# A hand-written order for the start of a fused kernel's last layer, and earlier rooms for its weights

## The chip, the cores and the metric

The kernel runs on one core of one Trainium2 chip. The metric is the time of one execution in device microseconds (us); the kernel before took 681.94 us (median of three runs, 681.19 to 682.96). A core has a matrix engine (TensorE, PE in the profile; its weight loads are PEld), a vector engine (VectorE, DVE), a scalar engine (ScalarE, ACT), GpSimd (POOL) and SyncE (SP), which here only issues DMAs. Each engine works through its own queue in order and waits at semaphores for the others. PSUM is the memory that PE writes to, SBUF the large working memory.

## The reference

Attention over 4 batches, 8 heads, 576 positions and 64 channels, then a soft mixture of experts, then a layer with the Mish function:

```python
x = attn_out.transpose(0, 2, 1, 3).reshape(2304, 512)
logits = x @ phi                              # 2304 x 32 slots
d = softmax over tokens; slot_input = d.T @ x # 32 x 512, four slots for each of 8 experts
slot_out[e] = relu(slot_input[e] @ w1[e]) @ w2[e]      # 512 -> 1024 -> 512
c = softmax over slots;  x = c @ slot_out     # 2304 x 512
h = x @ w_in                                  # 512 -> 2048
g = h * tanh(softplus(h))                     # Mish
out = g @ w_out                               # 2048 -> 512
```

`w_in` and `w_out` come as 64-bit floats, all else as 32-bit.

## The kernel before

**Stages.** Attention (to about 390 us), in which `w_in` is also converted to 32 bits and parked in DRAM; the experts (to 434 us); the last layer (to the end). The experts' weights are 32 loads of 1 MB, which go into tiles called rooms: `take` gives a room to the next key of a fixed list, `fetch` issues its DMA, `used` is called when the matmuls of a room stand in the program and gives the room to the next key. Rooms lie in the pools `ra` (5), `rd` (9), `rc` (3) and `rb` (`NRB` = 6). Once the experts' keys are all given out, `used` keeps a room of `ra`, and of `ra` alone, for the last layer (L144).

**Experts.** `h_ps` (L810) is the first expert layer, `so_ps` (L843) the second, in four quarters of 32 matmul rows in the profile. Between the quarters `combine` (L821) transposes the combine weights: PE writes `m_ct`, ACT copies it into `ct`, rounded to the matmul's short form, and DVE replaces two of four 32-row stripes by the remainder. So a matmul over 128 rows gives a product of nearly full precision. `so_ps` is then copied by DVE into `so_sb` (in the memory of `si_t`, L853), turned by PE (`m_sot`, L856) and copied by DVE to `s_t` (L857).

**Last layer.** `(c @ slot_out) @ w_in` is computed as `c @ (slot_out @ w_in)`. `inner(j)` makes 256 columns of `slot_out @ w_in`: matmuls `m_wp` (L911), ACT's copy `wp` (L913), a matmul `m_w` that repeats it over four stripes (L915), ACT's copy to `wst` (L917) and DVE's remainder (L918). `mish(u)` is one unit (256 tokens by 256 hidden columns): two matmuls `hp` (L932), Mish on ACT into `gg` (L938), a rounded copy `gh` (L940) and the remainder `gl` on DVE (L941). `second(u)` is that unit's share of the output: 12 matmuls `o_ps` (L957), of `gh` and `gl` with the two parts `wo_h` and `wo_l` of `w_out`. There are 72 units, in three groups of three token blocks by eight column blocks; a group ends with copies `ob` (L962) and stores.

`outer(c)` converts 128 rows of `w_out`, a chunk, from raw 64-bit words: ACT scales the words (L497, L498), DVE makes the number in five instructions (L503, L504, L505, L509, L510), ACT rounds it to `wo_h` (L896), DVE takes the remainder `wo_l` (L897). The 16 chunks are converted during the first group, through four raw buffers.

**What sets the order.** In the attention it is a plan written out; elsewhere a scheduler orders each engine's instructions by its own estimates, except those marked `tc.keep_in_program_order`. The program's text around the change:

```python
LOOK = 4
outer(0); outer(1); inner(0)
for u in range(len(units) + LOOK):
    if u < len(units): mish(u)    # in the first group also loads, outer(..) and inner(j + 1)
    if u >= LOOK: second(u - LOOK)
```

Of the kernel before, what the change touches and what calls it, by code (L numbers as in the profile page):

```python
# [42 lines left out]
def kernel(  # L43
# [23 lines left out]
    NRA, NRB, NRC = 8, 6, 3  # L67
# [28 lines left out]
    rd = late.enter_context(tc.tile_pool(name="rd", bufs=1, side="right"))  # L96
# [666 lines left out]
    ct = p2.tile([128, NT], F32R, name="ct")  # L763
# [56 lines left out]

    def combine(b):  # L821

        for t0, nt in ((0, 4), (4, 1)):
            ps = ps_m.tile([128, nt, 128], F32, tag="m", name="m_ct")
            for j in range(nt):
                for o in range(0, 128, 32):
                    nc.tensor.matmul(ps[o:o + 32, j, :], lhsT=c_all[:, b, t0 + j], rhs=ident, start=True, stop=True)
            n = 512 if nt == 4 else R
            src = ps.rearrange("p t n -> p (t n)")[:, 0:n]
            dst = ct[:, b * S + t0 * 128:b * S + t0 * 128 + n]  # L830
            nc.scalar.copy(dst, src)
            for o in (32, 96):
                nc.vector.tensor_tensor(out=dst[o:o + 32], in0=src[o:o + 32], in1=dst[o:o + 32].bitcast(F32),
                                        op=ALU.subtract)
# [18 lines left out]
    nc.vector.tensor_copy(so_sb, so_ps)  # L853
# [3 lines left out]
    nc.vector.tensor_copy(s_t, ps)  # L857
# [11 lines left out]
    p6 = ctx.enter_context(tc.tile_pool(name="p6", bufs=3, reuse_waits="tile"))  # L869


    raws = []
    for i in range(4):
        if i % 2:
            t = rooms[i][0].tile([128, 2048], U32, tag=rooms[i][1], name="raw")
            raws += [t[:, 0:1024], t[:, 1024:2048]]
        else:
            take(*rooms[i])
    for i in range(2):
        take(p3, f"wi{i}")  # L880

    def load_out(c):

        if c < NFC:
            tc.keep_in_program_order(
                nc.sync.dma_start(out=raws[c % 4], in_=w_out[c * 128:(c + 1) * 128, :].bitcast(U32)))

    def outer(c):

        t = raws[c % 4]  # L890
        w = p6.tile([128, DM], F32, tag="w", name="w", bufs=2)
        sg = p6.tile([128, DM], U32, tag="sg", name="sg", bufs=2)
        scale_words(t)
        high_word(t, sg, w.bitcast(U32))
        low_word(nc.vector, t, sg, w)
        nc.scalar.copy(wo_h[c], w)  # L896
        nc.vector.tensor_tensor(out=wo_l[c], in0=w, in1=wo_h[c].bitcast(F32), op=ALU.subtract)  # L897

    for x in (0, "i0", 1, 2, 3, "i1"):
        if isinstance(x, int):  # L900
            load_out(x)
        else:
            fetch((3, int(x[1]), 0), behind=True)

    def inner(j):

        fb, o = divmod(j * 256, 512)
        wi = parts[3, fb, 0][0].rearrange("p (c f) -> p c f", c=KDM)[:, :, o:o + 256]
        ps = ps_p.tile([128, 256], F32, tag="p", name="m_wp")
        for c in range(KDM):  # L910
            nc.tensor.matmul(ps[32 * c:32 * c + 32, :], lhsT=s_t[:, c, :], rhs=wi[:, c, :], start=True, stop=True)  # L911
        wp = p6.tile([128, 256], F32, tag="wp", name="wp", bufs=2)
        nc.scalar.copy(wp, ps)  # L913
        ps = ps_p.tile([128, 256], F32, tag="p", name="m_w")
        nc.tensor.matmul(ps, lhsT=rr, rhs=wp, start=True, stop=True)  # L915
        dst = wst[:, j * 256:(j + 1) * 256]
        nc.scalar.copy(dst, ps)  # L917
        nc.vector.tensor_tensor(out=dst[64:128], in0=ps[64:128], in1=dst[64:128].bitcast(F32), op=ALU.subtract)  # L918
# [8 lines left out]
    def mish(u):  # L927
        i, j = units[u]
        hp = ps_p.tile([128, 2, 256], F32, tag="p", name="hp")
        for x in range(2):  # L930
            f = 2 * j + x
            nc.tensor.matmul(hp[:, x, :], lhsT=wst[:, f * 128:(f + 1) * 128], rhs=ct[:, i * 256:(i + 1) * 256],  # L932
                             start=True, stop=True)
        hp = hp.rearrange("p a n -> p (a n)")
        gg = p6.tile([128, 512], F32, tag="gg", name="gg")
        gh = p6.tile([128, 512], F32R, tag="gh", name="gh", bufs=LOOK + 1)
        gl = p6.tile([128, 512], F32R, tag="gl", name="gl", bufs=LOOK + 1)
        nc.scalar.activation(out=gg, in_=hp, func=AF.Mish)  # L938
# [7 lines left out]
    def second(u):  # L946
        i, j = units[u]
        gh, gl = gs.pop(u)
        for n in range(2):
            if j == 0:  # L950
                ops[i, n] = ps_o.tile([128, DM], F32, tag="o", name="o_ps")
            ps = ops[i, n]
            for x in range(2):
                f = 2 * j + x
                cols = slice(x * 256 + n * 128, x * 256 + n * 128 + 128)
                for k_, (g_, w_) in enumerate(((gh, wo_h), (gh, wo_l), (gl, wo_h))):
                    nc.tensor.matmul(ps, lhsT=g_[:, cols], rhs=w_[f], start=(j == 0 and x == 0 and k_ == 0),  # L957
                                     stop=(j == NG - 1 and x == 1 and k_ == 2))
            if j == NG - 1:
                ob = p6.tile([128, DM], F32, tag="ob", name="ob", bufs=3)  # L960
                ps = ops.pop((i, n))
                (nc.scalar.copy if n else nc.vector.tensor_copy)(ob, ps)  # L962
                store(2 * i + n, ob)
# [17 lines left out]
    outer(0)  # L981
    outer(1)
    inner(0)
    for u in range(len(units) + LOOK):
        if u < len(units):
            mish(u)
            g, j = units[u][0] // GR, units[u][1]
            i = units[u][0] % GR
            if g == 0:
                if i < 2:  # L990
                    load_out(2 * j + 4 + i)
                if i == 0 and j % 2 == 0 and 2 + j // 2 < NFB:
                    fetch((3, 2 + j // 2, 0), behind=True)
                if j + 1 < NG:
                    if i < 2:
                        outer(2 * j + 2 + i)
                    if i == 1:
                        inner(j + 1)
        if u >= LOOK:
            second(u - LOOK)  # L1000
# [51 lines left out]
```

## Time and profile before

| | |
|---|---|
| median of three runs | 681.94 us |
| the profiled execution | 679.22 us |
| its span in the profile | 677.3 us |
| PE busy | 626.2 us (92%) |
| DVE busy | 404.9 us (60%) |
| ACT busy | 332.7 us (49%) |
| chain that ended last: PE | 77% |
| its line of most time, `o_ps` L957 | 28% |

The span is the time from the first to the last instruction that the profiler recorded on this core. A matmul's recorded duration overlaps with the next matmul's, so the distance of starts (the pitch) tells more than the busy share. The granted clock is the share of full speed, 2.4 GHz, at which TensorE was let run: 1.0, or 0.5 for 1.2 GHz.

### The profile page before, as it was taken

The page shows a single profiled execution, that of the slowest core. Times are in us where ns is not written, and L with a number is a line of the kernel's source. Part 1 is how long each engine was busy: PE and PEld are TensorE (multiplying, and loading weights), DVE is VectorE, ACT ScalarE, POOL GpSimd, SP SyncE. Part 2 cuts the span into 40 slices and gives each one's busy share as a digit, 9 for nine tenths or more (in the row PEclk, how much of TensorE's full clock was granted, in tenths as well). Part 3 has the DMA queues.
Part 4 walks back from the last instruction along what each step waited for, and adds up shares of the span by engine and source line. Part 5 has one row for each costly group of instructions (what it writes and reads, how often), then busy time and mean ns, then how long its engine had stood idle before and what let it go on. Part 6 is the DMA issues. An engine that isn't in the chain of part 4 may idle for free.

```text
span 677.3 us, 11071 instructions
## 1 busy us (share of the span) xinstructions
PE 626.2 (92%) x4002; PEld 461.1 (68%) x4002; DVE 404.9 (60%) x833; ACT 332.7 (49%) x755; POOL 206.8 (31%) x255
## 2 busy tenths in 40 slices
PE   1588899979999999999999998779999999999997
PEld 1565677657677777677677653357787888888885
DVE  6778677784775665656665421599973533343331
ACT  2556766763667656656565301288744321221221
POOL 5659759745675345424300010000000000000000
PEclk9999999998999999999999999969999999999999
DMA  9677689867596775346559579974300300030003
GB/s 265 158 208 186 190 263 270 205 219 199 157 291 183 189 215 130 90 112 172 129 181 315 185 267 379 339 266 164 125 1 0 94 1 0 1 94 0 1 0 94
DMA packets 58454, 107.32 MB, mean 158 GB/s; under 512 B 12704, under 2 KB 25120, under 8 KB 57888
## 3 DMA queue, kind: packets, MB, share of 16 engines
q1 hardware_dynamic: 58400, 106.62, 52.8%
q8 instruction: 32, 0.52, 0.4%
q14 instruction: 22, 0.18, 0.1%
HBM read 69.21 MB, written 8.91 MB: 115 GB/s over the span
## 4 chain that ended last, share of the span: by engine, by line
PE 77%; DMA 7%; DVE 5%; ACT 5%; SPq 2%; issue 2%; POOL 2%; ACTq 0%; DVEq 0%; POOLq 0%
PE o_ps L957 28%; PE m_av L426 14%; PE t L371 8%; PE s L330 5%; PE s L332 4%; PE s L350 3%; DMA w<-in_moe_w_in_dram 3%; PE hp L932 2%; PE so_ps L843 2%; DMA raw<-in_moe_w_out_dram 2%; PE m_lg L452 2%; SPq L185 1%; DMA w<-in_moe_w_dram 1%; PE tk L385 1%; ACT P L364 1%
## 5 line engine op out<-in xcount | busy, mean ns | idle before, releaser
L358 DVE TENSOR_REDUCE nmax<-s 128x1 f32<-128x576 f32 x144 | 108.2, 753 | 66.8 <-PE s L332 38.8
L364 ACT ACTIVATE P<-s,nmax 128x576 f32<-128x576 f32 x144 | 107.3, 745 | 28.2 <-DVE nmax L358 20.5
L957 PE MATMUL o_ps<-wo_h,gh 128*128 128x512 f32 x288 | 114.9, 399 | 0.8 <-ACT gh L940 0.8
L957 PE MATMUL o_ps<-wo_l,gh 128*128 128x512 f32 x288 | 113.9, 396 | 0.0
L957 PE MATMUL o_ps<-wo_h,gl 128*128 128x512 f32 x288 | 108.4, 391 | 0.0
L330 PE MATMUL s<-qk_st 128*128 128x288 f32 x256 | 85.6, 349 | 13.3 <-ACT P L364 7.8
L938 ACT ACTIVATE gg<-hp 128x512 f32<-128x512 f32 x72 | 42.3, 599 | 103.6 <-PE hp L932 100.9
L371 PE MATMUL t<-cs,P 128*128 128x128 f32 x512 | 79.5, 283 | 6.0 <-DVE partl L270 3.3
L407 ACT COPY PT<-t 128x512 f32<-128x512 f32 x93 | 54.2, 586 | 53.4 <-PE t L371 53.0
L371 PEld LDWEIGHTS t<-cs,P 128*128 128x128 f32 x512 | 59.9, 144 | 23.1 <-issue 11.6
L426 PE MATMUL m_av<-PT,w 128*64 128x320 f32 (+1 forms) x384 | 73.1, 421 | 0.9 <-ACT PT L396 0.6
L332 PE MATMUL s<-k_st,qk_st 128*128 128x288 f32 x256 | 73.4, 301 | 0.0
L330 PEld LDWEIGHTS s<-qk_st 128*128 128x128 f32 x256 | 49.7, 194 | 31.0 <-ACT P L364 11.5
L940 DVE CAST gh<-gg 128x512 fp32r<-128x512 f32 x48 | 20.5, 427 | 75.0 <-ACT gg L938 75.0
L228 POOL TENSOR_TENSOR w<-w,cs 128x512 f32<-128x512 f32 x34 | 45.6, 1343 | 61.9 <-PE m_k L282 53.6
L957 PEld LDWEIGHTS o_ps<-wo_h,gh 128*128 128x128 f32 x288 | 54.8, 190 | 13.8 <-ACT gh L940 2.9
L957 PEld LDWEIGHTS o_ps<-wo_h,gl 128*128 128x128 f32 x288 | 54.2, 188 | 11.7 <-DVE sg L509 0.4
L957 PEld LDWEIGHTS o_ps<-wo_l,gh 128*128 128x128 f32 x288 | 54.9, 191 | 9.3
L941 DVE TENSOR_TENSOR gl<-gg,gh 128x512 fp32r<-128x512 f32 x72 | 49.4, 690 | 8.9 <-ACT gh L940 4.4
L332 PEld LDWEIGHTS s<-k_st,qk_st 128*128 128x128 f32 x256 | 49.9, 195 | 0.0
L225 POOL TENSOR_TENSOR w<-w,cs 128x512 f32<-128x512 f32 x34 | 44.5, 1308 | 8.3 <-DMA w<-in_k_dram 3.8
L426 PEld LDWEIGHTS m_av<-PT,w 128*64 128x64 f32 x384 | 26.6, 136 | 22.2 <-issue 9.0
(172 smaller groups left out, 995.6 us busy)
## 6 DMA issues: line engine op xcount, KB each, us to landing
w<-in_moe_w_dram SPq DMA_DIRECT2D x28, 1024.0 KB, 7.6
w<-in_moe_w_in_dram SPq DMA_DIRECT2D x16, 512.0 KB, 6.8
raw<-in_moe_w_out_dram SPq DMA_DIRECT2D x16, 512.0 KB, 4.1
qk_st<-parth SPq DMA_DIRECT2D x46, 144.0 KB, 3.2
qk_st<-partl SPq DMA_DIRECT2D x46, 144.0 KB, 3.2
w<-in_q_dram SPq DMA_DIRECT2D x16, 256.0 KB, 5.5
w<-in_k_dram SPq DMA_DIRECT2D x16, 256.0 KB, 4.7
w<-in_moe_w_dram SPq DMA_DIRECT2D x16, 256.0 KB, 5.6
```

Source lines behind the costliest of these rows:

```text
L225: eng.tensor_tensor(out=tb, in0=src, in1=sin.to_broadcast([128, n, w]), op=ALU.mult)
L228: eng.tensor_tensor(out=dst, in0=sv, in1=cv, op=ALU.mult)
L330: nc.tensor.matmul(s[:, half, 0:288], lhsT=st[:, qc:qc + 128], rhs=st[:, KC + o:KC + o + 288], start=first, stop=False)
L332: nc.tensor.matmul(s[:, half, 0:288], lhsT=st[:, qc:qc + 128], rhs=k2_st[p % 2][:, o:o + 288], start=False, stop=last)
L358: nc.vector.tensor_reduce(out=stat[p][0][:, i:i + 1], in_=s[:, :, 0:288], axis=AX.XY, op=ALU.max, negate=True)
L364: nc.scalar.activation(out=P[p, t][:, h * S:(h + 1) * S].rearrange("p (a b) -> p a b", a=2), in_=s[:, :, 0:288], func=AF.Exp, bias=stat[p] ...
L371: nc.tensor.transpose(ps[:, j, :], P[p, t][:, blk * 128:(blk + 1) * 128], ident)
L407: nc.scalar.copy(dst, src)
L426: nc.tensor.matmul(ps[o:o + 64, :], lhsT=lhsT, rhs=rhs, start=(c == 0), stop=(c == 4))
L938: nc.scalar.activation(out=gg, in_=hp, func=AF.Mish)
L941: nc.vector.tensor_tensor(out=gl, in0=gg, in1=gh.bitcast(F32), op=ALU.subtract)
L957: nc.tensor.matmul(ps, lhsT=g_[:, cols], rhs=w_[f], start=(j == 0 and x == 0 and k_ == 0), stop=(j == NG - 1 and x == 1 and k_ == 2))
```

## The change

Rooms: a seventh room in `rb`; `rd` lives as long as `ra`, and `used` keeps rooms of both. The four raw buffers, the first inner weights, most of the combine weights (`ct` is cut in two at column 1792), and the small buffers of conversion and Mish are now such rooms, and the loads of four raw chunks and of the first inner weights are issued right behind the experts' weights.

Order: almost every instruction from `combine` on is marked `pin`, that is `tc.keep_in_program_order`. `cv(c, k)` is one step of a chunk's conversion; chunks 0 and 1 are converted ahead of the copy of `so_ps`, which is halved between DVE and ACT and followed by two warm-up matmuls. `inner` is split into `inner_a` and `inner_b`. In the first group `mish` places four conversion steps per unit, `second` takes its four `gl` matmuls last, and it runs one unit behind `mish` at first and four units later on, `min(LOOK, 1 + u // 4)`.

```diff
-    NRA, NRB, NRC = 8, 6, 3
+    NRA, NRB, NRC = 8, 7, 3
...
-    rd = late.enter_context(tc.tile_pool(name="rd", bufs=1, side="right"))
+    rd = ring.enter_context(tc.tile_pool(name="rd", bufs=1, side="right"))
...
-        elif room[0] is ra:
+        elif room[0] in (ra, rd):
             rooms.append(room)
...
+    for x in (0, 1, "i0", 2, 3):
+        if x == "i0":
+            fetch((3, 0, 0), behind=True)
+        else:
+            load_out(x)
...
-    nc.vector.tensor_copy(so_sb, so_ps)
+    for c in range(2):
+        cv(c, "S")
+        for k in range(1, 6):
+            cv(c, k)
+    for eng, cols in ((nc.vector.tensor_copy, slice(0, DM // 2)), (nc.scalar.copy, slice(DM // 2, DM))):
+        pin(eng(so_sb[:, cols], so_ps[:, cols]))
+    warm(ps_m, "m", 2)
...
+    def stream():
+
+        for c in range(2, NFC):
+            yield c, 1
+            yield c, 2
+            yield c - 1, "L"
+            yield c, 3
+            if c + 1 < NFC:
+                yield c + 1, "S"
+            yield c, 4
+            load_out(c + 4)
+            yield c, 5
+            yield c, "H"
+        yield NFC - 1, "L"
...
+        if u < NG * GR:
+            convert(4 if u else 2)
+        pin(nc.vector.tensor_tensor(out=gl, in0=gg, in1=gh.bitcast(F32), op=ALU.subtract))
...
+        if u < NG * GR:
+
+            todo.sort(key=lambda y: y[2] == 2)
...
-    outer(0)
-    outer(1)
-    inner(0)
...
+    cv(0, "H")
+    cv(1, "H")
+    cv(0, "L")
+    cv(2, "S")
+    inner_a(0)
+    convert(1)
+    inner_b(0)
+    convert(1)
+    done = 0
+    for u in range(len(units)):
...
+        mish(u)
+        if g == 0 and j + 1 < NG:
+            if i == 0:
+                inner_a(j + 1)
+            elif i == 1:
+                inner_b(j + 1)
+
+        while done < u + 1 - min(LOOK, 1 + u // 4):
+            second(done)
+            done += 1
```

On DVE, at the end of the experts, the built program had this (`ct` are the combine weights, `si_t` the copy of `so_ps`):

```order
L833 TENSOR_TENSOR ct<-m_ct,ct 32x64 x2
L853 COPY si_t<-so_ps 128x512
L857 COPY s_t<-m_sot 128x128
L503 TENSOR_SCALAR sg<-raw 128x512
L504 SCALAR_TENSOR_TENSOR w<-raw,sg 128x512
L505 TENSOR_SCALAR sg<-w 128x512
L509 TENSOR_TENSOR sg<-sg,raw 128x512
L510 TENSOR_TENSOR w<-w,sg 128x512
```

and now has this (every buffer in a kept room is called `room`; L861 to L870 are a chunk's five steps):

```order
L893 TENSOR_TENSOR ct_4498<-m_ct,ct_4498 32x64 x2
L861 TENSOR_SCALAR room<-room 128x512
L863 SCALAR_TENSOR_TENSOR room<-room 128x512
L866 TENSOR_SCALAR room<-room 128x512
L868 TENSOR_TENSOR room<-room 128x512
L870 TENSOR_TENSOR room<-room 128x512
L861 TENSOR_SCALAR room<-room 128x512
L863 SCALAR_TENSOR_TENSOR room<-room 128x512
L866 TENSOR_SCALAR room<-room 128x512
L868 TENSOR_TENSOR room<-room 128x512
L870 TENSOR_TENSOR room<-room 128x512
L918 COPY si_t<-so_ps 128x256
```

The copy of `so_ps`, now half as wide, moved from right behind the combine weights to behind two chunks of conversion. On ACT, from the last combine copy to the first Mish, the order was:

```order
L831 CAST ct<-m_ct 128x64
L497 ACTIVATE raw<-raw 128x512
L498 ACTIVATE raw<-raw 128x512
L896 CAST wo_h_4843<-w 128x512
L913 COPY wp<-m_wp 128x256
```

and is now, from the second chunk's scaling on:

```order
L858 ACTIVATE room<-room 128x512
L859 ACTIVATE room<-room 128x512
L918 COPY si_t<-so_ps 128x256
L872 CAST wo_h_4874<-room 128x512
L872 CAST wo_h_4875<-room 128x512
L858 ACTIVATE room<-room 128x512
L859 ACTIVATE room<-room 128x512
L974 COPY room<-m_wp 128x256
L981 CAST wst<-m_w 128x256
L1003 ACTIVATE room<-hp 128x512
L1005 CAST gh<-room 128x512
```

The copy `wp` (L974) moved from behind one rounding to behind ACT's half of the copy, two roundings and a third chunk's scalings; in the built program ACT's L918 waits for DVE's L918, and the first L872 for the last `m_sot`. On SP, around the last expert loads, the order was:

```order
L135 DMA w_7_1_4588<-in_moe_w_dram 128x512
L886 DMA raw<-in_moe_w_out_dram 128x1024
L135 DMA w_0_0_4879<-scr_in 128x2048
L886 DMA raw<-in_moe_w_out_dram 128x1024 x3
L135 DMA w_1_0_4881<-scr_in 128x2048
```

and is now:

```order
L135 DMA w_7_1_4572<-in_moe_w_dram 128x512
L844 DMA room<-in_moe_w_out_dram 128x1024 x2
L135 DMA w_0_0_4646<-scr_in 128x2048
L844 DMA room<-in_moe_w_out_dram 128x1024 x4
L135 DMA w_1_0_4910<-scr_in 128x2048
```

The second raw load moved ahead of the first inner weights, and the fifth and sixth ahead of the second.

## Rows read from the trace of the kernel before

**Rows 1.** Chain of waits, in order of time: start us, us, what.

```profile
426.33 3.43 PE so_ps L843 x32
...
432.41 7.84 DMA raw<-in_moe_w_out_dram
...
444.62 0.81 PE hp L932 x2
```

**Rows 2.** Timeline of PE: start us, us, engine, line, op, tiles, shapes, count.

```profile
430.89 3.62 PE L843 MATMUL so_ps<-w,h_t 128*32 128x512 f32 x32
435.49 1.05 PE L856 MATMUL m_sot<-cs,si_t 128*128 128x32 f32 x8 [0.98 <-DVE si_t L853]
438.14 1.08 PE L911 MATMUL m_wp<-w,s_t 128*32 128x256 f32 x8 [1.59 <-DVE w L504]
441.07 1.22 PE L915 MATMUL m_w<-wp,cs 128*128 128x256 f32 x2 [1.85 <-ACT wp L913]
...
447.12 0.80 PE L957 MATMUL o_ps<-wo_h,gh 128*128 128x512 f32 x1
...
450.70 0.57 PE L957 MATMUL o_ps<-wo_h,gl 128*128 128x512 f32 x1
```

**Rows 3.** Timeline of DVE, same columns.

```profile
430.30 0.46 DVE L833 TENSOR_TENSOR ct<-m_ct,ct 32x64 fp32r<-32x64 f32 x2 [1.06 <-ACT ct L831]
431.54 1.87 DVE L833 TENSOR_TENSOR ct<-m_ct,ct 32x512 fp32r<-32x512 f32 x4 [0.79 <-ACT ct L831]
434.65 0.69 DVE L853 COPY si_t<-so_ps 128x512 f32<-128x512 f32 x1 [1.25 <-PE so_ps L843]
436.58 0.29 DVE L857 COPY s_t<-m_sot 128x128 f32<-128x128 f32 x1 [1.23 <-PE m_sot L856]
436.90 0.43 DVE L503 TENSOR_SCALAR sg<-raw 128x512 uint32<-128x512 uint32 x1
...
439.35 0.69 DVE L510 TENSOR_TENSOR w<-w,sg 128x512 f32<-128x512 f32 x1
```

**Rows 4.** Timeline of ACT, same columns.

```profile
440.13 0.62 ACT L896 CAST wo_h<-w 128x512 fp32r<-128x512 f32 x1 [5.61 <-DVE w L510]
440.65 0.36 ACT L913 COPY wp<-m_wp 128x256 f32<-128x256 f32 x1
440.92 0.68 ACT L497 ACTIVATE raw<-raw 128x512 f32<-128x512 f32 x1
441.49 0.67 ACT L498 ACTIVATE raw<-raw 128x512 f32<-128x512 uint32 x1
...
445.46 1.08 ACT L938 ACTIVATE gg<-hp 128x512 f32<-128x512 f32 x2 [0.79 <-PE hp L932]
```

**Rows 5.** Half-microsecond windows: PE busy, then the granted clock, DMA share, GB/s.

```profile
437.00:437.50 0.50, 0.00 (x0) 0.91 0.95 377
...
451.00:451.50 0.50, 0.50 (x3) 0.94 0.06 25
```

**Rows 6.** SP's DMA issues, in a timeline.

```profile
429.78 0.33 SPq L886 DMA_DIRECT2D raw<-in_moe_w_out_dram  x1
```

**Rows 7.** Chain of waits, in the last layer's steady part.

```profile
635.19 2.75 PE o_ps L957 x12
637.93 0.23 PE hp L932 x2
```

**Rows 8.** Timeline of PE, its last matmul.

```profile
672.26 0.39 PE L957 MATMUL o_ps<-wo_h,gl 128*128 128x512 f32 x1
```

**Rows 9.** Timeline of PE, `m_wp` between `o_ps`.

```profile
467.59 0.64 PE L911 MATMUL m_wp<-w,s_t 128*32 128x256 f32 x8
468.16 0.50 PE L957 MATMUL o_ps<-wo_h,gl 128*128 128x512 f32 x1
```

**Rows 10.** PE's waits from 447 to 530 us: us, times, longest.

```profile
PE o_ps L957 <- ACT gh L940: 0.8, 2, 0.6
```

**Rows 11.** Windows of 10 us: PE, PEld, DVE, ACT, POOL busy; clock, DMA share, GB/s.

```profile
460.00:470.00 10.00, 10.00 (x52) 7.75 (x52) 9.60 (x19) 8.26 (x18) 0.00 (x0) 1.00 0.42 139
```

More of the change, by code (lines that the diff above doesn't have):

```diff
@@ L819, with room, load_out, cv @@
     tc.keep_in_program_order(nc.scalar.preload_act_table_set("mish"))
+    def room(dtype):
+        pool, tag = rooms.pop(0)
+        return pool.tile([128, 2048], dtype, tag=tag, name="room")
+    rt = [room(U32) for _ in range(2)]
+    raws = [t[:, o:o + 1024] for t in rt for o in (0, 1024)]
+    take(*rooms.pop(0))
+    cts[0] = room(F32R)
+    wt, gt = room(F32), room(F32)
+    ws3 = [wt[:, i * DM:(i + 1) * DM] for i in range(3)]
+    sg = wt[:, 3 * DM:4 * DM].bitcast(U32)
+    ggs = [gt[:, i * 512:(i + 1) * 512] for i in range(3)]
+    wps = [gt[:, 1536 + i * 256:1792 + i * 256] for i in range(2)]
+    pin = tc.keep_in_program_order
+    def load_out(c):
+        if c < NFC:
+            pin(nc.sync.dma_start(out=raws[c % 4], in_=w_out[c * 128:(c + 1) * 128, :].bitcast(U32)))
+    for x in (0, 1, "i0", 2, 3):
[3 more added lines that the diff above has]
+            load_out(x)
+    def cv(c, k):
+        lo, hi = words(raws[c % 4])
+        w = ws3[c % 3]
+        wb, sf = w.bitcast(U32), sg.bitcast(F32)
+        if k == "S":
+            pin(nc.scalar.activation(out=hi.bitcast(F32), in_=hi.bitcast(F32), func=AF.Copy, scale=2.0 ** -112))
+            pin(nc.scalar.activation(out=lo.bitcast(F32), in_=lo, func=AF.Copy, scale=2.0 ** -52))
+        elif k == 1:
+            pin(nc.vector.tensor_scalar(out=sg, in0=hi, scalar1=0x80000000, scalar2=None, op0=ALU.bitwise_and))
+        elif k == 2:
+            pin(nc.vector.scalar_tensor_tensor(out=wb, in0=hi, scalar=3, in1=sg, op0=ALU.logical_shift_left,
+                                               op1=ALU.bitwise_or))
+        elif k == 3:
+            pin(nc.vector.tensor_scalar(out=sg, in0=wb, scalar1=0xFF800000, scalar2=None, op0=ALU.bitwise_and))
+        elif k == 4:
+            pin(nc.vector.tensor_tensor(out=sf, in0=sf, in1=lo.bitcast(F32), op=ALU.mult))
+        elif k == 5:
+            pin(nc.vector.tensor_tensor(out=w, in0=w, in1=sf, op=ALU.add))
+        elif k == "H":
+            pin(nc.scalar.copy(wo_h[c], w))
+        else:
+            pin(nc.vector.tensor_tensor(out=wo_l[c], in0=w, in1=wo_h[c].bitcast(F32), op=ALU.subtract))
     def combine(b):
@@ L829, in combine @@
             src = ps.rearrange("p t n -> p (t n)")[:, 0:n]
[L830 to L834, printed above, removed]
+            a = b * S + t0 * 128
+            m = min(max(CTA - a, 0), n)
+            for x, y, t, w in ((0, m, 0, a), (m, n, 1, a - CTA)):
+                if x == y:
+                    continue
+                d = cts[t][:, w + x:w + y]
+                pin(nc.scalar.copy(d, src[:, x:y]))
+                for o in (32, 96):
+                    pin(nc.vector.tensor_tensor(out=d[o:o + 32], in0=src[o:o + 32, x:y],
+                                                in1=d[o:o + 32].bitcast(F32), op=ALU.subtract))
     so_ps = ps_m.tile([128, DM], F32, tag="m", name="so_ps")
@@ L869, with convert, inner_a @@
     p6 = ctx.enter_context(tc.tile_pool(name="p6", bufs=3, reuse_waits="tile"))
[L872 to L905, printed above, removed]
+    for _ in range(3):
+        take(*rooms.pop(0))
+    for c in (4, 5):
+        load_out(c)
+    fetch((3, 1, 0), behind=True)
+    def stream():
[11 more added lines that the diff above has]
+        yield NFC - 1, "L"
+    steps2 = stream()
+    def convert(n):
+        while n:
+            x = next(steps2, None)
+            if x is None:
+                return
+            cv(*x)
+            n -= x[1] not in ("S", "H")
+    def inner_a(j):
         fb, o = divmod(j * 256, 512)
@@ L980 @@
     LOOK = 4
-    outer(0)
-    outer(1)
-    inner(0)
[L984 to L1000, printed above, removed]
+    cv(0, "H")
[8 more added lines that the diff above has]
+    for u in range(len(units)):
+        g, j = units[u][0] // GR, units[u][1]
+        i = units[u][0] % GR
+        if g == 0 and i == 2 and j in (0, 2):
+            fetch((3, 2 + j // 2, 0), behind=True)
+        mish(u)
[7 more added lines that the diff above has]
+            done += 1
+    while done < len(units):
+        second(done)
+        done += 1
     ring.close()
```

52 lines of the change are left out of this document (26 added, 26 removed).

## The prediction

> **What bounds the kernel now.** I read the chain of waits first, from 426 us on. Through the expert stage it names PE alone; then it goes over a DMA of raw words to `hp`, and back to PE for good [rows 1]. The timeline of PE gives the ends of that stretch: the last `so_ps`, 430.89 + 3.62 = 434.51, and the first `o_ps`, 447.12 [rows 2]. Late in the last layer a unit is 12 `o_ps` in 2.75 and two `hp` in 0.23 us, 2.98 without idle time [rows 7], to the last `o_ps` at 672.26 [rows 8]. So what moves the start of `o_ps`, or leaves PE idle after it, is paid in full; what DVE and ACT save besides is not.
>
> 72 units of 2.98 are 214.6, of which the 0.46 of two units' `hp` was done before 447.12. Seven later blocks of first-layer weights cost 0.57 for `m_wp` (467.59 to 468.16 [rows 9]) and about 0.23 for `m_w`, taken as a pair of `hp`, less one 0.57 done already: 5.0. Ideal 219.2; from 447.12 to 672.26 + 0.39 there are 225.5, so 6.3 us are lost after the start, in the first group, since later units show none. The clock explains 1.9 of them: it was granted at 1.0 until about 437.4 and at 0.5 until 451.1 [rows 5], and nine `o_ps` took 4.0 us in place of 2.1, a pitch of about 0.45 [rows 2].
>
> The 12.6 us ahead of `o_ps`, by rows 2 to 4: DVE copies `so_ps` (434.65, 0.69), PE turns it (435.49, 1.05), DVE copies `s_t` (436.58), and `m_wp` runs at 438.14. Then ACT is late: `wp` (440.65) stands behind `wo_h`, which waits 5.6 for DVE's conversion; `m_w` is at 441.07, ACT's `wst` stands behind four scalings, and Mish starts at 445.46. What stretches it is the order on two queues, and DMAs issued only from 429.78 on [rows 6].
>
> **The change, part by part.** *Rooms and DMAs.* The raw and inner weights go into rooms that the experts' first layer leaves before `so_ps` starts, so SP issues them right behind the last expert weight and waits no more for the third quarter of `so_ps`, after which the first raw load was issued in before [rows 6]. A seventh room lets one expert load go earlier. I price both at 0: the chain through `so_ps` names PE and no load [rows 1], so no expert weight is late; and the first conversions, which want the raw words, cannot start before DVE is free, below. Were the loads 5 us late after all, they would still be in time.
>
> *DVE's order.* This decides. In before DVE ends the combine weights at 431.54 + 1.87 = 433.41 and is free for `so_ps`. In the changed program ten instructions, two chunks of conversion, stand between, and DVE works in its queue's order. The combine tile cut at column 1792 adds a pair of 64-column subtractions, 0.46 [rows 3]: free at 433.9. A chunk's five instructions ran from 436.90 to 440.04, 3.14 us [rows 3], since each reads the one before; two chunks are 6.3: 440.2. Half the copy, 256 columns, lies between the 0.29 of 128 columns and the 0.69 of 512 [rows 3]; I take 0.42: 440.6. ACT's half waits for DVE's in the built program; 0.36 as `wp` [rows 4]: 441.0. Half of the 1.05 of `m_sot` is left after it: 441.5. `s_t`, 0.29: 441.8. `m_wp`, 1.08 at half clock: 442.9.
>
> The Trainium skill, "PSUM — Partial Sum Buffer", section "PSUM bank collisions raise a hardware error", says that two engines must not be in the same bank and partitions at once, even at different columns, and that software has to order them. The built order agrees: the halved copy takes 0.42 + 0.36 end to end, where one copy took 0.69 [rows 3]. Were the halves side by side, the sum below would be 0.4 less.
>
> *ACT's order.* `wo_h` of chunk 0 now waits for `m_sot`, since its memory lay under the copied tile: 441.5. Behind it stand a second cast, at a pitch of 0.52 (440.13 to 440.65), and two scalings of chunk 2 at 0.57 [rows 4], 2.2 in all, and only then `wp`: 443.7 to 444.1. `m_w` 1.22 [rows 2]: 445.3. `wst` 0.36 on ACT and 0.42 on DVE: 446.2. From `hp` to Mish 0.84 [rows 1, 4]: 447.0. A Mish, 0.6 (two took 1.08 [rows 4]): 447.6. The second `hp` needs the buffer that this Mish reads, `m_w` of block 1 stands behind it, and then `o_ps`: 0.4, half of the chain's 0.81 [rows 1], and, at half clock, between 0.5 and the 1.22 of a whole `m_w`, about 0.9: 449.0. That is **1.9 later** than 447.12. PE then has that `m_w` behind it: **-0.2**. Bounds of the start: with the clock at full speed the PE pieces here lose half, 1.6, so +0.3; with 0.1 more at each of some fifteen hand-overs, +3.4. I keep 1.9, since nearly every step has a row.
>
> *Two warm-up matmuls* stand after `so_ps`. In before the clock fell after 2.9 us that held only `m_sot` (434.51 to 437.4 [rows 2, 5]); in the changed order the 6 us to 440.6 hold only these two, some tenths long. I take the clock as low through the chain, and its return as long after the first `o_ps` as in before, 4.0 us: **0**. Bounds: it returns at the first `o_ps`, -1.9; 3 us later, +1.5. The Trainium skill, "TensorE: Matmul & The Clock Gate", section "Why this matters for your kernels", asks for matmul bursts without long idle gaps, or the clock falls. By it the two matmuls hold nothing and the sum stays; if they held the clock, the sum would be about 3.5 less. The trace agrees as far as it goes [rows 5].
>
> *First group by hand.* Of the 4.4 us that are not the clock's, the waits of `o_ps` for `gh` are 0.8 [rows 10]; I let these go. Against that, the distance between the two products grows from one unit to four inside the group: three times PE does two `hp` with no `o_ps` between them, and waits for a Mish of 0.6 that ran beside `o_ps`. After `m_wp` or `m_w` standing there I leave 0.4 of each: 1.2. Net **+0.4**; bounds -4.4, every loss gone, and +5, from a rival below. The group's DVE and ACT work is the same but for the two chunks done ahead. The other two groups stay at 2.98 a unit, since PE is never idle there.
>
> Sum: 1.9 - 0.2 + 0 + 0.4 = +2.1. The profiled execution took 679.22 (a span of 677.3 and 1.9 around it) and would take 681.3. The timed median, 681.94, lies 2.7 above it, so I forecast **684.0**.
>
> **Rivals.** *The group gives the late start back* (0.26). DVE comes out of the chain with two chunks done, so conversions never hold PE; half of the 4.4 goes, and the time is 682, no change. For it: DVE is 96% busy in 460 to 470 [rows 11]. Against it: PE hardly waited for DVE.
>
> *Faster* (0.13). All of the 4.4 goes: -4.4 + 1.7 = -2.7, 679.2. Or the conversions fill DVE's idle time during the experts, as the change's order suggests, and the copy finds DVE free at 434.6: then the chain is 5.6 shorter and the time 678. Against the second: all ten stand behind the last combine subtraction, which started at 431.54 and whose input PE makes.
>
> *The hand order becomes the bound* (0.11, slower). The place is DVE in the first group. Three units hold two chunks, 2 x (3.14 + 0.6), three `gl` of 0.6 and one `wst` of 0.42: 9.7 us, with 0.6 for a 512-column instruction behind an independent one (an estimate from durations of 0.69 [rows 3]). PE needs 3 x 2.98 + 0.80 = 9.7. They are level, and in a fixed queue a wait is not made up. It decides once DVE has used up the lead of four units; 0.2 us a unit over 24 units is 5: 688 with the late start.
>
> *As forecast* (0.50): a later start and a group as lossy as before, 682.6 to 686.2.
>
> **How the numbers follow.** About 0.3%, 2 us, is what a measurement of this kernel tells from no change. The forecast sits on that edge: its 0.50 is 0.30 slower and 0.20 same, since late hand-overs only add. Half given back: 0.22 same, 0.02 faster, 0.02 slower. Faster: 0.11 and 0.02 same. Bound by hand order: 0.11 slower. Together faster 0.13, same 0.44, slower 0.43. The range 679.4 to 688.0 reaches into the faster case and to the price of the slower one and leaves about a tenth out on either side.
>
> **What would show it.** In the profile after: DVE's half of `si_t` near 440, PE without work for about 5 us before `m_sot`; `wp` behind two casts and two scalings on ACT; the first `o_ps` near 449; a granted clock of 0.5 from about 437 to 453; raw words there before 433. I am wrong if `si_t` is copied before 437, if the clock stays up, or if the end moves by what the first group lost or saved after its start and not by the start.

## The result

The changed kernel takes 690.04 us (median of four runs, 687.50 to 690.38) against 682.20 for before beside it: a ratio of 1.0108, 95% interval 1.0080 to 1.0135, slower. Forecast were 684.0 and a range of 679.4 to 688.0; the time lies 2.0 outside. Run again later, it took 688.85, ratio 1.0106 (1.0071 to 1.0141).

### The profile page after: what moved, and what is told of

Its sections match the earlier page's. It is cut to its first block, busy times and chain, and to the rows that moved or that the text cites. A ratio compares the mean times of both kernels' runs of the same rounds, so it can differ in the third digit from the quotient of the medians.

```text
span 688.0 us, 11063 instructions
## 1 busy us (share of the span) xinstructions
PE 632.4 (92%) x4006; PEld 465.4 (68%) x4006; DVE 406.2 (59%) x835; ACT 336.0 (49%) x757; POOL 206.9 (30%) x255
## 4 chain that ended last, share of the span: by engine, by line
PE 81%; DVE 8%; DMA 4%; ACT 3%; issue 2%; POOL 1%; SPq 1%; DVEq 0%; ACTq 0%; POOLq 0%
PE o_ps L1027 28%; PE m_av L426 14%; PE t L371 8%; PE s L330 6%; PE s L332 4%; PE s L350 3%; PE hp L996 2%; PE h_ps L812 2%; DMA w<-in_moe_w_in_dram 2%; PE m_lg L452 2%; PE so_ps L903 2%; PE m_k L282 1%; PE tk L385 1%; PE m_q L282 1%; ACT P L364 1%
## 5 line engine op out<-in xcount | busy, mean ns | idle before, releaser
L1027 PE MATMUL o_ps<-wo_h,gl 128*128 128x512 f32 x288 | 101.0, 391 | 0.0
L1003 ACT ACTIVATE room<-hp 128x512 f32<-128x512 f32 x72 | 43.1, 599 | 118.4 <-PE hp L996 118.3
L371 PEld LDWEIGHTS t<-cs,P 128*128 128x128 f32 x512 | 60.2, 144 | 23.2 <-issue 10.7
L426 PE MATMUL m_av<-PT,w 128*64 128x320 f32 (+1 forms) x384 | 74.7, 429 | 0.7 <-ACT PT L396 0.5
L1005 DVE CAST gh<-room 128x512 fp32r<-128x512 f32 x48 | 20.5, 428 | 80.0 <-ACT room L1003 80.0
L1027 PEld LDWEIGHTS o_ps<-wo_h,gl 128*128 128x128 f32 x288 | 54.1, 188 | 11.7
L1008 DVE TENSOR_TENSOR gl<-room,gh 128x512 fp32r<-128x512 f32 x72 | 49.7, 691 | 9.3 <-ACT gh L1005 4.0
```

What stands on the lines that cost most here:

```text
L371: nc.tensor.transpose(ps[:, j, :], P[p, t][:, blk * 128:(blk + 1) * 128], ident)
L426: nc.tensor.matmul(ps[o:o + 64, :], lhsT=lhsT, rhs=rhs, start=(c == 0), stop=(c == 4))
L1003: pin(nc.scalar.activation(out=gg, in_=hp, func=AF.Mish))
L1008: pin(nc.vector.tensor_tensor(out=gl, in0=gg, in1=gh.bitcast(F32), op=ALU.subtract))
L1027: pin(nc.tensor.matmul(ops[i, n], lhsT=g_[:, cols], rhs=w_[f], start=(j == 0 and (x, k) == (0, 0)), stop=(j == NG - 1 and all(y[0] != n fo ...
```

## The profile after

The profiled execution took 690.0 us, its span is 688.0, so 10.7 more than before's 677.3. I divide it at two places: the end of the last `so_ps` and the first `o_ps`. PE's timeline of the changed kernel answers to [rows 2] (start us, us, engine, line, op, tiles, shapes, count, idle time before and what ended it):

```profile
434.68 3.62 PE L903 MATMUL so_ps<-w,h_t 128*32 128x512 f32 x32
438.23 0.71 PE L548 MATMUL warm<-cs 128*128 128x128 f32 x4
445.11 1.89 PE L922 MATMUL m_sot<-cs,si_t 128*128 128x32 f32 x8 [6.16 <-DVE si_t L918]
447.38 1.08 PE L973 MATMUL m_wp<-w,s_t 128*32 128x256 f32 x8 [0.38 <-DVE s_t L923]
449.66 1.22 PE L979 MATMUL m_w<-room,cs 128*128 128x256 f32 x2 [1.20 <-ACT room L974]
451.80 0.80 PE L996 MATMUL hp<-room,wst 128*128 128x256 f32 x2 [0.92 <-DVE wst L982]
...
454.87 0.81 PE L1027 MATMUL o_ps<-wo_h,gh 128*128 128x512 f32 x1
```

The last `so_ps` starts at 434.68, in before at 430.89: 3.8 of the 10.7 are lost ahead of everything the change touches. From its end (434.68 + 3.62 = 438.30) to the first `o_ps` it is 16.57, in before 12.61: 3.96 more. From the first `o_ps` to the end of the last it is 228.50 (683.37), in before 225.54: 2.96 more. These three make the 10.7.

The start, on DVE, answers to [rows 3] (same columns):

```profile
436.02 1.73 DVE L893 TENSOR_TENSOR ct<-m_ct,ct 32x448 fp32r<-32x448 f32 x4 [0.60 <-ACT ct L891]
437.79 0.43 DVE L861 TENSOR_SCALAR room<-room 128x512 uint32<-128x512 uint32 x1
...
439.86 0.69 DVE L868 TENSOR_TENSOR room<-room 128x512 f32<-128x512 f32 x1 [0.46 <-DVE room L866]
...
443.81 0.69 DVE L870 TENSOR_TENSOR room<-room 128x512 f32<-128x512 f32 x1
444.54 0.42 DVE L918 COPY si_t<-so_ps 128x256 f32<-128x256 f32 x1
447.03 0.29 DVE L923 COPY s_t<-m_sot 128x128 f32<-128x128 f32 x1 [2.07 <-PE m_sot L922]
```

The ten instructions of two chunks fill DVE from 437.79 to 444.50, and the copy that PE has waited for since 438.95 comes behind them. On ACT, against [rows 4]:

```profile
444.99 0.37 ACT L918 COPY si_t<-so_ps 128x256 f32<-128x256 f32 x1 [6.57 <-DVE si_t L918]
447.08 1.14 ACT L872 CAST wo_h<-room 128x512 fp32r<-128x512 f32 x2 [1.72 <-PE m_sot L922]
448.13 0.66 ACT L858 ACTIVATE room<-room 128x512 f32<-128x512 f32 x1
...
449.24 0.37 ACT L974 COPY room<-m_wp 128x256 f32<-128x256 f32 x1
...
452.64 0.60 ACT L1003 ACTIVATE room<-hp 128x512 f32<-128x512 f32 x1 [1.35 <-PE hp L996]
```

`wp` (L974) stands behind two casts and two scalings, as laid out, and Mish (L1003) follows 3.0 behind it. The clock, against [rows 5] (windows: PE, PEld, DVE, ACT, POOL busy, then the granted clock):

```profile
438.30:441.60 3.30, 0.64 (x4) 0.45 (x4) 2.69 (x5) 0.12 (x1) 0.00 (x0) 1.00 0.12 48
441.70:455.30 13.60, 7.69 (x33) 4.61 (x34) 7.84 (x16) 5.65 (x12) 0.00 (x0) 0.50 0.40 151
455.40:479.20 23.80, 21.52 (x113) 16.38 (x114) 21.39 (x38) 19.10 (x37) 0.00 (x0) 1.00 0.49 171
479.30:482.60 3.30, 3.30 (x14) 2.01 (x11) 3.20 (x7) 2.19 (x5) 0.00 (x0) 0.50 0.67 262
```

It is low through the chain, as priced, and back 0.5 us after the first `o_ps`, not 4.0; but it falls once more at 479. At half clock `o_ps` follow each other at a pitch of about 0.45 us [rows 2] and at full clock at 0.23 (12 in 2.75 [rows 7]), so half of the time that PE works at half clock is lost: behind the first `o_ps` (0.47 + 3.4) / 2 = 1.9 us here and 4.0 / 2 = 2.0 in before. It explains none of the 2.96. PE's waits from 454 to 500 us do, against the 0.8 of [rows 10] (us, times, longest):

```profile
PE hp L996 <- DVE wst L982: 2.0, 2, 1.7
PE m_w L979 <- ACT room L974: 0.9, 1, 0.9
PE hp L996 <- ACT room L1003: 0.3, 1, 0.3
```

With a small one, 3.3 us, in five places, all between 465 and 493, at units 4 to 13, and all ahead of `hp` or `m_w`, none ahead of `o_ps`; three of them:

```profile
465.85 0.50 PE L996 MATMUL hp<-room,wst 128*128 128x256 f32 x2 [0.26 <-ACT room L1003]
...
478.75 0.47 PE L996 MATMUL hp<-room,wst 128*128 128x256 f32 x2 [1.72 <-DVE wst L982]
...
493.07 0.70 PE L979 MATMUL m_w<-room,cs 128*128 128x256 f32 x2 [0.94 <-ACT room L974]
```

The chain of waits says what lies behind the longest, 1.72 (start us, us, what):

```profile
467.04 0.44 DVE room L861
...
478.18 0.44 DVE wst L982
...
478.75 0.47 PE hp L996 x2
...
484.31 0.23 PE hp L996 x2
484.54 0.43 PE m_w L979 x2
```

From 467.04 to 478.62 it names 20 instructions of DVE and no other engine, with no gap over 0.1 us: here DVE is behind, and PE waits for it. A wait also costs something beside itself: the `hp` behind it takes 0.47 and the `m_w` 0.70, where they take 0.23 and 0.43 without one.

## Experiments

My theory had two parts. A: the late start is the order on two queues, DVE's ten conversions ahead of the copy and ACT's casts and scalings ahead of `wp`. G: the group's waits stand where the distance between a unit's two products grows. Rival D: DVE's sum of work sets the group's pace. The distance is the number of units by which `second` runs behind `mish`. A measure that the attention does not disturb is used throughout: the start (end of `so_ps` to first `o_ps`) and the stretch (first `o_ps` to the end of the last).

**The copy alone first.**

```diff
     for c in range(2):
         cv(c, "S")
-        for k in range(1, 6):
-            cv(c, k)
...
     pin(nc.vector.tensor_copy(s_t, ps))
+    for c in range(2):
+        for k in range(1, 6):
+            cv(c, k)
```

> The changed kernel with one move on VectorE: the two halves of the so_ps copy and the s_t copy stand ahead of the ten conversion instructions, not behind them. All other queues are as in the changed kernel. Theory A (the first o_ps is late because of the order on two queues, VectorE's ten conversions ahead of the copy and then ScalarE's two casts and two scalings ahead of wp): the copy starts within 0.5 us of the end of so_ps (now 6.2 behind it), but wp still waits on ScalarE for two casts that need both chunks, so only 1 to 1.5 us come back: first o_ps about 15.3 us behind the end of so_ps (now 16.6), time about 689. Rival B (VectorE's place of the copy is the whole price): the start gives back the 6 us, first o_ps about 10.5 behind so_ps, time about 684. Rival C (the lost time is in the first group and at the clock, not at the start): time stays within 0.7 of the changed kernel's whatever the start does.

Measured: 686.63 us, ratio 1.0078 (1.0060 to 1.0096); start 15.79, stretch 227.36. PE's timeline, `m_sot` and `m_w`:

```profile
438.08 1.05 PE L920 MATMUL m_sot<-cs,si_t 128*128 128x32 f32 x8
...
447.93 1.22 PE L980 MATMUL m_w<-room,cs 128*128 128x256 f32 x2 [7.78 <-ACT room L975]
```

The 6.16 ahead of `m_sot` are gone and stand, as 7.78, ahead of `m_w`: `wp` waits on ACT for casts of both chunks. Only 0.8 us of the start came back, less than the 1 to 1.5 that I wrote; the stretch is 1.1 shorter since the clock did not fall a second time in it (1.3 us at half clock in place of 3.9). Rival B falls, and so does C's number, since the time moved by 2 us by the two ratios; the two queues are one obstacle.

**Copy first, and every step where PE asks for it.**

The edit has some thirty lines; in words, the new orders are these:

- DVE: copy, 2 steps of chunk 0, `s_t`, 3 steps, 2 of chunk 1, `wst`, 3 steps, `wo_l`.
- ACT: copy, `wp`, `wo_h[0]`, `wst`, Mish 0, `gh` 0, `wo_h[1]`, scalings of chunk 2.
- SP: the load into chunk 1's raw words behind that chunk's last step.

> The changed kernel with the copy of so_ps first, and each later step in the order in which PE asks for it: on VectorE two conversion steps, s_t, the rest of chunk 0, two steps of chunk 1, wst, the rest; on ScalarE wp ahead of the casts, wst behind the first cast, Mish ahead of the second cast and the scalings. Theory A: the start comes back, first o_ps about 8.5 us behind the end of so_ps (changed kernel 16.6, before 12.6), and the time falls by 6 to 8 us to 682 to 684. Rival B (what bounds the start is the sum of VectorE's work on two chunks, some 9 us, wherever it stands): first o_ps not under 12, time 686 or more. Rival C (loss in the first group): the start comes earlier but PE then waits longer for VectorE inside the group, and the time falls by less than 3.

Measured: 683.78 us, ratio 1.0026 (1.0006 to 1.0047); start 10.41, 6.2 earlier than the changed kernel and 2.2 earlier than before; stretch 229.76. Theory A holds, though 8.5 was 1.9 too short: `m_w` of block 1, ahead of the first `o_ps`, still waited 1.50 for `wp` behind the two scalings. The stretch has the changed kernel's waits (0.26, 0.30, 1.69, 0.12, 0.94), and half clock in 6.4 us of it: without the clock's share 226.6, as there (228.50 - 1.9). So the start's gain is kept to the end and rival C falls.

**In the group, weights of the first layer ahead of the conversions.**

```diff
         if u < NG * GR:
+            if j + 1 < NG:
+                if i == 0:
+                    inner_a(j + 1)
+                elif i == 1:
+                    inner_b(j + 1)
             convert(4 if u else 2)
...
         mish(u)
-        if g == 0 and j + 1 < NG:
...
```

> The changed kernel with the first group's first-layer weights ahead of the conversions: in a unit that makes wp or wst, ScalarE copies wp or wst right behind the cast of gh, and VectorE subtracts for wst ahead of that unit's conversion steps, not behind them. The start is as in the changed kernel (16.6 behind so_ps). Theory A (the group loses 3.3 us of PE idle time in waits for wst and wp, 1.72 at the longest, and 1.7 more by the half clock that follows the longest): both go, time 685 to 687. Rival (the sum of VectorE's work bounds the group, so the wait only moves to gl or wo_l): the idle time reappears at o_ps and the time stays within 1 of the changed kernel's.

Measured: 687.37 us, ratio 1.0096 (1.0076 to 1.0116); start 16.58, stretch 229.42. My theory's number failed. No `hp` waits for `wst` any more, but at the same step `m_wp` waits for the Mish that frees its PSUM buffer:

```profile
476.32 0.64 PE L973 MATMUL m_wp<-w,s_t 128*32 128x256 f32 x8 [1.90 <-ACT room L1003]
```

On ACT that Mish stands behind a cast that waited for DVE's conversion:

```profile
475.15 0.62 ACT L872 CAST wo_h<-room 128x512 fp32r<-128x512 f32 x1 [1.67 <-DVE room L870]
```

The chain of waits goes back from it over DVE alone, from 475.13 to 463.88. So the wait moved to the next thing wanted in the same place. It did not go to `gl` or `wo_l`, as the rival had it, but the rival's engine, DVE, is again the one that is behind.

**Before again.** No edit.

> The kernel before, unchanged, for its trace. In the changed kernel's trace so_ps comes 3.8 us later than in the trace of before, and that difference starts at 74 to 84 us, in the attention, where both programs have the same order: a weight load landed 1.1 us later, PE idled 3.4 in place of 2.1 and the granted clock was 0.5 for 6.8 us after it. Theory A (chance of an execution, not the change): this second trace of before has half clock in other places of the attention than the first, and so_ps starts at a time that differs by over 1 us from 416.3. Rival (a property of the changed program): the two traces of before agree within 0.5 us at so_ps, with half clock only at 31 and 151.

Measured: 682.26 us, ratio 1.0004 (0.9987 to 1.0021); span 680.84, start 12.61, stretch 225.39, but `so_ps` begins at 419.93 in place of 416.20. Windows of before, of this run, of the changed kernel and of the changed kernel run again (below); the first two are one program, the last two another:

```profile
75.60:82.50 6.90, 6.40 (x41) 3.89 (x42) 3.91 (x8) 5.85 (x15) 4.99 (x4) 1.00 0.18 57
```

```profile
75.60:82.50 6.90, 5.67 (x19) 3.06 (x19) 3.63 (x7) 5.08 (x13) 2.57 (x2) 0.51 0.02 8
```

```profile
75.60:82.50 6.90, 5.21 (x17) 2.69 (x18) 3.61 (x7) 5.53 (x14) 2.56 (x2) 0.56 0.05 19
```

```profile
75.60:82.50 6.90, 5.91 (x37) 3.40 (x37) 3.95 (x8) 6.33 (x16) 4.50 (x4) 1.00 0.15 43
```

Both programs have executions with and without half clock there, and the changed kernel run again begins `so_ps` at 416.26. The 3.8 us are chance of an execution.

**A distance of one unit throughout.**

```diff
-        while done < u + 1 - min(LOOK, 1 + u // 4):
+        while done < u:
```

> The changed kernel with one edit: the second product of a unit always follows the first product of the next one, so the distance of one unit stays, and does not grow to four at units 4, 8 and 12. The start is as in the changed kernel (first o_ps 16.6 us behind so_ps). Theory G (PE's 3.3 us of idle time between 465 and 493 stand at the steps where the distance grows, since there two hp follow each other with no o_ps between to cover wst, wp or Mish): the waits of hp and m_w in the group go, none of over 0.5 is left, the clock does not fall again in the group, and first to last o_ps takes 224 to 226 us in place of 228.5; time 3 to 4.5 lower than the changed kernel's 690.0. Rival D (VectorE's sum of work sets the group's pace, my third rival before the result): the idle time comes back as waits of o_ps for gh, gl or wo_l, and the stretch stays at 228 to 230.

Measured: 684.04 us, ratio 1.0032 (1.0007 to 1.0057) where the changed kernel has 1.0106, so 5 us of the 7, a little more than I wrote; start 16.56, stretch 223.66. PE waits for nothing in the group. A window inside it, of the changed kernel and then of this one:

```profile
474.80:484.80 10.00, 8.28 (x38) 6.01 (x36) 9.67 (x18) 6.61 (x14) 0.00 (x0) 0.83 0.56 211
```

```profile
476.40:486.40 10.00, 10.00 (x53) 7.95 (x52) 8.93 (x17) 7.50 (x14) 0.00 (x0) 1.00 0.56 209
```

DVE does the same work, 8.93 in 10, while PE is never idle, so its sum alone is not the bound. Theory G holds, and D as a pace that the sum sets at any distance falls: where the distance grows, two `hp` follow with no twelve `o_ps` between, and the 2.75 us that covered `wst`, `wp` or Mish are not there.

What is left of D sizes the waits. Four units are 13.5 us of PE's work (four times 2.98 and 4/3 of the 1.2 that a block's weights cost, see below), so 12.1 of DVE's at this run's share. A growth step takes 2.75 out of PE's part and nothing out of DVE's, and leaves DVE 1.3 behind: 3.9 in three steps, against 3.3 us of waits measured. That is an estimate, and it leaves out the waits that end on ACT; no run made DVE's sum smaller, two made it larger (below).

The clock's share can be taken off as well, half of the time at half clock behind the first `o_ps`. What is left of the stretch is 226.6 to 226.7 in five traces with the growing distance (the changed kernel's two, the first, second and last run), 223.5 in both traces of before and 222.3 here. So the growing distance costs 4.3 against a constant one, 3.3 of it in waits.

**`wo_l` on GpSimd.**

```diff
-            pin(nc.vector.tensor_tensor(out=wo_l[c], ...
+            pin((nc.gpsimd if c > 1 else nc.vector).tensor_tensor(out=wo_l[c], ...
```

> The changed kernel with one edit: from chunk 2 on the subtraction that makes wo_l is done on GpSimd, idle until then, and no more on VectorE, which is relieved of 14 instructions of 0.69, 9 to 10 us over the group of 72. All else, the growing distance too, stays. Rival D (VectorE's sum of work sets the group's pace): first to last o_ps falls by 2.5 us or more, the 1.7 us wait of hp for wst at unit 9 is under 0.5, and the time is 3 or more lower. Theory G (the steps of the distance): VectorE has idle time instead, the waits at the steps shrink by what VectorE's queue was late there, some tenths, and the time moves by less than 1.5.

Measured: 692.87 us, ratio 1.0184 (1.0147 to 1.0220), slower than the changed kernel; stretch 233.82. It does not tell D from G, since DVE was not relieved. Lines of the changed kernel's first group, then of this run's (busy us, mean ns of one):

```profile
L1008 DVE TENSOR_TENSOR gl<-room,gh 128x512 fp32r<-128x512 f32 x20 | 13.7, 685 | 0.0
```

```profile
L874 POOL TENSOR_TENSOR wo_l<-room,wo_h 128x512 fp32r<-128x512 f32 x13 | 19.8, 1520 | 101.8 <-ACT wo_h L872 101.8
L1009 DVE TENSOR_TENSOR gl<-room,gh 128x512 fp32r<-128x512 f32 x19 | 19.6, 1034 | 1.1 <-ACT gh L1006 1.1
```

The means mix two kinds. A `gl` that meets one of POOL's subtractions takes up to 1.82 us, the others 0.68 as before:

```profile
487.61 1.30 POOL L874 TENSOR_TENSOR wo_l<-room,wo_h 128x512 fp32r<-128x512 f32 x1 [4.76 <-ACT wo_h L872]
```

```profile
487.64 1.82 DVE L1009 TENSOR_TENSOR gl<-room,gh 128x512 fp32r<-128x512 f32 x1
```

With DVE slower the waits for `wst` grew from 2.0 to 5.2.

**Start and distance together.** The second run's order, `while done < u`, and `wp` of block 1 ahead of the second cast on ACT.

> The kernel of the second run (copy first, ScalarE in the order PE asks) with the distance of one unit throughout, and wp of block 1 ahead of the second cast on ScalarE. Theory A with G: first o_ps 9.0 to 9.5 us behind so_ps (10.4 there), first to last o_ps 225 to 226.5, so the time is 676 to 679, 3 to 6 us under before. Rival D: first to last o_ps stays near 229.8 or grows, since the start comes earlier and VectorE has no lead: 682 to 684, no change against before.

Measured: **674.14 us, ratio 0.9905 (0.9873 to 0.9936), faster than both kernels**; start 8.79, stretch 223.61. What PE waits for from 433 to 530 us:

```profile
PE hp L998 <- DVE wst L984: 1.3, 1, 1.3
PE m_w L981 <- ACT room L976: 0.5, 1, 0.5
PE m_wp L975 <- DVE s_t L923: 0.4, 1, 0.4
PE o_ps L1036 <- DVE gl L1015: 0.2, 1, 0.2
```

Start, stretch and time all came out below what I wrote. Against before the start is 3.8 and the stretch 1.9 shorter, 5.7 in sum, where the ratio makes 6.5: the two gains add up. Of the 1.9, 1.2 is the clock, at half for 1.5 us behind the first `o_ps` in place of 4.0, and 0.6 is waits.

**The same with `wo_l` on GpSimd.** The edit of the sixth run on top.

> The same kernel with wo_l from chunk 2 on made on GpSimd, which takes 9 to 10 us of work off VectorE in the group. Theory G: with the steps of the distance gone VectorE's sum is not the bound, and this is within 1 us of the run before it. Rival D: 2.5 us or more under the run before it.

Measured: 678.92 us, ratio 0.9952 (0.9927 to 0.9977), 4.8 over the run before it; stretch 227.36, in which PE now waits 2.0 for `gl`. Both numbers failed, for the reason above. It shows how little room DVE has: with some of its instructions slower it holds PE even at the constant distance.

**The changed kernel again.** No edit.

> The changed kernel once more, for its time beside before on one chip and for a second trace. If the 3.8 us by which so_ps came later in its first trace are chance, so_ps starts anywhere between 415 and 421.5 (the spread of the traces so far, of both programs), while first o_ps behind so_ps (16.6) and first to last o_ps (228.5) come out within 0.5 and 1.5 of the first trace. By these two the change costs 3.96 + 3.1 = 7.1 us, a ratio of 1.0104; if the 3.8 belonged to the change it would be 10.9, a ratio of 1.016.

Measured: 688.85 us, ratio 1.0106 (1.0071 to 1.0141); `so_ps` begins at 416.26, start 16.58, stretch 228.17. The clock did not fall at 479 here, but stayed at half 3.1 us past the first `o_ps`. Start and stretch repeat. Against the second trace of before, this trace is 3.97 + 2.8 longer in the two and the first 3.96 + 3.1, so 6.8 to 7.1 us; the ratio, 1.06% of 681.7, makes 7.2.

**A distance of four from the first unit.**

```diff
-        while done < u + 1 - min(LOOK, 1 + u // 4):
+        while done < u + 1 - LOOK:
```

> The changed kernel with the distance of four units from the first unit on, as the program text of before has it: PE does four first products, each behind a Mish, before the first o_ps, and the distance does not grow in the group. Theory G: the start is later by three more units of Mish and cast on ScalarE, about 1.2 each, so first o_ps about 20 us behind so_ps, and the group runs without the five waits, first to last o_ps 223 to 225; the sum, about 244, is 1 us under the changed kernel's 245.1, time about 689. Rival (with four units in hand ScalarE and VectorE fall behind anyway): first to last o_ps 227 or more, time 692 or more.

Measured: 688.91 us, ratio 1.0105 (1.0076 to 1.0134); start 24.28, stretch 222.81. The group has no waits, as G has it. The stretch is the shortest of all, in part because three `hp` pairs, an `m_wp` and an `m_w` more lie ahead of the first `o_ps`, about 1.7 us at full clock. The start was 4 later than I wrote, so start and stretch are 2.0 longer than the changed kernel's and not 1 shorter; the fourth unit needs block 1:

```profile
457.77 0.77 PE L996 MATMUL hp<-room,wst 128*128 128x256 f32 x2 [2.72 <-DVE wst L982]
```

**The best kernel without `gl` last.**

```diff
-            todo.sort(key=lambda y: y[2] == 2)
```

> The kernel of the seventh run (start and distance) with the order of the twelve matmuls of a unit of the first group as it was in before: the product with gl third and not at the end of the unit. In the trace of the seventh run gl ends 1.1, 2.1 and 1.6 us behind the first o_ps of units 0 to 2 and 0.3 to 0.8 behind it in most later ones, and in this order PE wants it 0.46 behind. Theory (gl at the end is what lets PE run without idle time at a distance of one unit): PE waits for gl in units 0 to 5, about 2 us in sum, since a wait early leaves less for a later one; first to last o_ps about 225.6 in place of 223.6, time about 676. Rival (the order is worth nothing): no wait over 0.2, the same time as the seventh run.

Measured: 678.81 us, ratio 0.9954 (0.9934 to 0.9973), 4.7 over the best, or 3.3 by the two ratios; stretch 226.15, start 8.51. The waits for `gl` sum to 1.9, 1.62 of it in one place:

```profile
451.66 0.50 PE L1036 MATMUL o_ps<-wo_h,gl 128*128 128x512 f32 x1 [1.62 <-DVE gl L1015]
```

This part of the change is worth the 2.5 us of the stretch, of which 1.7 are waits. The medians were taken on two chips; by the ratios, each with before beside it, the difference is within their intervals of that.

**The changed kernel without the warm-ups.** `warm(ps_m, "m", 2)` taken out.

> The changed kernel without the two warm-up matmuls behind so_ps. I priced them at nothing: the granted clock fell 3.4 us behind so_ps with them (2.9 in before without), and PE has no other work until the copy comes, 6.8 us behind so_ps. If that holds, the clock falls at the same place within one us, first o_ps stays 16.6 behind so_ps and the time is within 1 us of the changed kernel's. Rival (they carry the clock into the chain for part of the way): the fall comes 1 to 3 us earlier and the start is later by some tenths up to 1 us.

Measured: 688.80 us, ratio 1.0101 (1.0077 to 1.0125); start 16.57, stretch 229.42. The clock fell 5.2 us behind `so_ps` here, later and not earlier, and the start is the same. The rival falls, and the price of nothing holds.

## Why the prediction was wrong

**The start: right in mechanism, 2.1 too short.** Behind the end of `so_ps`, forecast from before's rows and then measured in the changed kernel's trace:

| until | forecast | measured |
|---|---|---|
| ten conversions done | 5.7 | 6.20 |
| both halves copied | 6.5 | 7.06 |
| `m_sot` done | 7.0 | 8.70 |
| `s_t` done | 7.3 | 9.02 |
| `wp` done | 9.2 to 9.6 | 11.31 |
| `wst` done on DVE | 11.7 | 13.45 |
| Mish starts | 12.5 | 14.34 |
| first `o_ps` | 14.5 | 16.57 |

The mis-sized term is `m_sot`. I took its 1.05 from [rows 2], where the clock was still up, though my own term for the warm-ups had the clock low by then; it took 1.89, and 1.64 of that lay behind ACT's half. That is 1.1 of the 2.1. A wait of 0.46 in the first chunk, put down to the preceding instruction of the same engine and the same in the four traces with this start (both of the changed kernel, distance four, no warm-ups), is another 0.5; no run shows why it is there. From `s_t` to Mish each step came within about 0.1 of its row; the last, to `o_ps`, took 0.2 more.

**The first group: the step that failed most.** I wrote "+0.4": 0.8 of waits let go, three growth steps of 0.4. The 0.8 went as said. The growth steps cost 3.3 in waits, and some 0.2 to 0.3 more at each wait, since I had only counted the second `hp`'s wait for a Mish, and not that `wst` and `wp`, two queues and four hand-overs long, lose the same cover, nor that DVE has too little time to spare to follow. Distance one shows it, with no wait left. With my -0.8 and -0.2 these terms make 3.3 to 3.8, where 2.96 was measured; what lies between is not placed.

**What could be won in the group was counted too high.** I took 0.23 for an `m_w` and nothing for the `o_ps` behind an `m_wp`. The chain of waits of before has 0.43, and 16 `o_ps` in 3.85 behind `m_wp` where they take 3.65 otherwise:

```profile
468.23 3.85 PE o_ps L957 x16
472.08 0.43 PE m_w L915 x2
...
472.75 3.65 PE o_ps L957 x16
```

That is 0.4 more for each of seven blocks, so 2.8 of the 4.4 that I called lost were work: the ideal is about 222, and distance one, with no wait, has 222.3 without the clock. The bound of -4.4 and both rivals that win part of it stood on this; the forecast hardly did.

**The rival of the hand order** had the place (DVE, `wst`), the sign and nearly the time, 688, and half of the cause. It counted 9.7 us for DVE and for PE in three units. Distance one has DVE at 8.93 in 10, so they are not level, and DVE's sum binds only where a growth step takes 2.75 out of PE's. The rival had the growing distance as a lead that DVE uses up; it is what makes DVE late. Of 0.11 it deserved more; my 0.4 a step counted one Mish alone.

**Clock, rooms, warm-ups: nothing, as priced.** From the first `h_ps` to the first `so_ps` it is 17.06 us in both programs (399.14 to 416.20, 402.93 to 419.99), and 18.31 from there to the end of `so_ps` (434.51, 438.30), so neither the seventh room nor the earlier raw words shorten or lengthen the experts. Behind the first `o_ps` the clock's share is 1.9 to 2.0 in the first trace of both. I had the return 4.0 behind `o_ps`; 0.5 and 3.1 were measured, and with the 0.5 it was luck that a second fall, which I had not forecast, made up for the early return.

**From the span to the time.** Adding 2.7, since the profiled execution was under its median, was right in direction: the second trace of before is 3.6 us longer by its attention alone. Of the 6.0 missed, 2.1 are the start, 2.8 the group (2.96 against the +0.4 - 0.2), and the last 1.1 is 3.8 less the 2.7, chance of one execution.

## What to carry to other kernels

A queue in fixed order is read from the consumer: whatever stands in it ahead of an instruction that another engine waits for is on the path, and moving one queue right can leave the wait to the next one. When a software pipeline's distance grows on the way, each step of growth takes one unit's cover from everything that was hidden behind it, and an engine that is 89% busy cannot make that up; choose a distance that holds from the first unit. Compare kernels by stretches between two events that both have: two executions of one program differed here by 3.7 us ahead of the change, half of what the change costs.

## What the runs showed of the hardware

The attention's length is a draw: from the start of the span to the first `so_ps` it took 415.0 to 421.5 us over fourteen traces with the same order there, with half clock at 76 to 82 us in some. In before that stretch stands behind an idle time of PE of 2.10 us, in the changed kernel's first trace behind 3.41, as the weight words that ACT waits for arrived later; in the first the clock stayed at 1.0:

```profile
74.11 0.65 ACT L497 ACTIVATE w<-w 128x512 f32<-128x512 f32 x1 [2.16 <-DMA w<-in_moe_w_in_dram]
```

```profile
75.30 0.65 ACT L497 ACTIVATE w<-w 128x512 f32<-128x512 f32 x1 [3.47 <-DMA w<-in_moe_w_in_dram]
```

VectorE is slower beside GpSimd: with `wo_l` on GpSimd a subtraction `gl` took 1034 ns on average in place of 685, up to 1.82 us where the two met and 0.68 elsewhere. The Trainium skill, "SBUF — State Buffer", section "Who interferes with whom", says that a VectorE instruction with two SBUF inputs contends with a GpSimd instruction that reads SBUF. The rows of the sixth run agree: `gl` and `wo_l` each read two tiles of SBUF.
